# Zeros matmuls, a moved group of transposes and a swapped FFN block in the first stage of an attention and max-out FFN kernel

## The chip, the cores and the metric

The kernel runs on one core of a Trainium2 chip. The metric is device time in microseconds: the median of several executions. Besides, one execution of the kernel is recorded by the hardware profiler; the views shown here come from that execution.

## The reference

Attention with a relative-position bias, followed by a feed-forward network whose hidden layer is the largest of three products. There are 8 batches, 8 heads, 576 positions and a head width of 64; the model width is 512 and the hidden width 768.

```python
scores = scale * np.matmul(q, k.transpose(0, 1, 3, 2))
...
bias = bias_table[bucket]                      # bucket depends on |i - j| alone
scores = scores + bias.transpose(2, 0, 1)[None]
attn = np.exp(scores - max); attn = attn / (sum + 1e-09)
x = (attn @ v), as (4608 tokens, 512)
h = np.maximum(np.maximum(x @ w1, x @ w2), x @ w3)
out = h @ w_out
```

## The kernel before

Heads are taken in pairs (`hp` from 0 to 3), since two heads of width 64 fill 128 partitions. For a pair, q and k are turned (head width onto partitions) into `qT` and `kT`; `scores` (line 793) multiplies two tiles of keys with 256 queries into a PSUM tile `sc` of the pool `ps_s`, and ScalarE takes the exponential of it (`exp`, line 776) into `e4`. The bias is not added: exponentials that lie in a band around the diagonal are multiplied by the exponential of the bias (`times_band`, line 767, reading `hank`), on VectorE. The last 64 keys and queries of the 576 are handled apart (`left_keys`, `left_queries`, tile `el`). `attend` (line 876) multiplies with v, a column of ones giving the sums, and `quotients` divides. The result `x_sb` is turned into `xT`, which the FFN reads.

The pool `ps_s` has two tiles of two banks; `ps_a` and `ps_f` have two tiles of one bank each. A new tile of a pool waits until the last reader of the tile that it replaces is done.

The order of the work on TensorE is the order of the program text: the helpers `mm` and `tr` (lines 106 and 110) keep it. VectorE's copies and band products are kept in program order as well (`inorder`), and so are the transfers on the queues of SP and POOL. The exponentials on ScalarE are placed by the framework in this stage.

Batch 0 is special, because nothing is loaded yet when it begins. It is worked in two passes, both over the four pairs (from line 1048 and from line 1080). The first pass does the first 256 queries: for a pair it calls `visit` (line 811; two groups of scores, with an optional call `mid` between them), turns the q and k of the next pair (`first_transposes`, line 712: six or seven TensorE transposes into `ps_f` tiles, then two VectorE copies), casts keys from float32, runs one matmul on zeros (`keep_warm`, line 1040) and, from the second pair on, the left keys. `last_keys` (line 729) turns the tails of k for the first two pairs. Ahead of all of it stand eight matmuls on zeros (line 292) and the bias product (`spread_bias`, line 298).

The second pass does the other 320 queries, multiplies with v, and begins on the FFN of batch 0. The FFN's work is cut into portions, each a list of functions with its number of matmuls per tile; `add_ffn` (line 662) puts them into a queue, and `fill(target)` (line 677) takes portions up to the target. Where `fill` is given a hook, it runs the hook before the last function that it took. For the first 256 tokens the portions are those of line 642: `f` are the products with the first weight (`first`, line 387: eight matmuls into a `ps_f` bank, then a ScalarE copy into `hT`), `m` those with the second (`second`, line 396: eight matmuls, then a VectorE maximum), `g` those with the third. The first `fill(8)`, line 1131, takes f[0]; the one of line 1144 takes the second portion, with the turning of batch 1's first pair as its hook.

The weights, batch 1's q and k, and v go through POOL's DMA queue, in the order of the text: w1 behind batch 0's v (line 1016), then parts of batch 1, w2 (line 1027), the rest of batch 1's q and k, batch 1's v, w3 (line 1030), batch 2.

## Time and profile before

| what | value |
|---|---|
| median of 3 runs | 313.13 us (313.09, 313.13, 316.0) |
| profiled execution, its own time | 312.26 us |
| its span, first to last instruction | 310.5 us |
| busy: TensorE, VectorE, ScalarE, POOL | 96%, 67%, 65%, 36% of the span |
| mean granted TensorE clock | 0.989 |
| chain that ended last | TensorE 89%, ScalarE 5%, DMA 2% |

Times in the views are microseconds from the start of the span, so the profiled execution's own time holds 1.8 us that lie outside it. "PE" is TensorE's matmuls, "PEld" its weight loads, DVE is VectorE, ACT is ScalarE. In a timeline each row is the start, the time, the engine, the line, the operation and its tiles, and in brackets how long the engine had been idle and what ended that. Most TensorE rows carry the lines of the helpers `mm` (L107) and `tr` (L111), so they are told apart by their tiles: `warm` and `idle` are the zeros, `tp` transposes, `sc` scores, `sct` left keys, `a` the products with v, `ps` the FFN's first products.

### The profile page before, as it was taken

What the parts mean: (1) busy time and instruction counts of PE and PEld (TensorE: products, weight loads), DVE (VectorE), ACT (ScalarE), POOL (GpSimd) and SP (SyncE); (2) the same over time, 40 slices, a digit from 0 to 9 for tenths busy, and PEclk for the clock granted to TensorE, in tenths of its full rate; (3) what the DMA queues carried; (4) which work ended last, traced back from release to release, by engine and by line L of the source; (5) the groups of instructions that cost most, each with busy time, mean ns of one, the idle gap of its engine ahead of it and who ended that gap; (6) DMA issues with size and microseconds to landing.
All of it is one profiled execution on the core that took longest, in us unless ns stands there. A gap on an engine that the chain in (4) does not pass through costs nothing.

```text
span 310.5 us, 10532 instructions
## 1 busy us (share of the span) xinstructions
PE 298.9 (96%) x4542; PEld 182.5 (59%) x4542; DVE 207.7 (67%) x475; ACT 202.4 (65%) x268; POOL 110.9 (36%) x147
## 2 busy tenths in 40 slices
PE   6989999999999999999999999989999999999995
PEld 2357777775555655657665756666667654444442
DVE  7389788776777776776777667766776665553552
ACT  3899988886778777767776877675776730122211
POOL 8978752951096008900647024901500000000000
PEclk9599999999999999999999999999999999999999
DMA  9999999999999999999999999999932014202003
GB/s 167 198 187 199 182 163 136 145 166 139 141 157 191 151 187 155 133 147 198 105 101 125 165 183 111 112 146 202 131 62 106 36 33 80 101 0 103 34 0 135
DMA packets 163950, 40.48 MB, mean 130 GB/s; under 512 B 153784, under 2 KB 159424, under 8 KB 163904
## 3 DMA queue, kind: packets, MB, share of 16 engines
q0 software_dynamic: 103840, 16.66, 75.7%
q1 hardware_dynamic: 58304, 22.69, 43.6%
q8 instruction: 35, 0.57, 0.8%
q10 hardware_dynamic: 1760, 0.47, 0.7%
q14 instruction: 11, 0.09, 0.1%
HBM read 35.39 MB, written 9.45 MB: 144 GB/s over the span
## 4 chain that ended last, share of the span: by engine, by line
PE 89%; ACT 5%; DMA 2%; issue 1%; DVE 1%; ACTq 1%; DVEq 0%
PE psp L107 34%; PE ps L107 19%; PE a L107 14%; PE sc L107 9%; PE pso L107 6%; ACT e L777 4%; PE sct L107 2%; PE scq L107 2%; PE tp L111 1%; DMA xT<-in_q_dram 1%; DMA out_dram<-osb 1%; ACT el L777 1%; ACTq L213 1%; PE xp L111 0%; DVE k_sb L124 0%
## 5 line engine op out<-in xcount | busy, mean ns | idle before, releaser
L777 ACT ACTIVATE e<-sc 128x1024 bf16<-128x1024 f32 x128 | 128.4, 1023 | 30.4 <-PE sc L107 27.3
L107 PEld LDWEIGHTS <-w_bf 64*128 64x128 bf16 (+1 forms) x1088 | 73.4, 95 | 57.9 <-issue 5.0
L107 PE MATMUL psp<-xT,w_bf 64*128 64x512 bf16 x736 | 91.9, 376 | 1.9 <-issue 1.8
L771 DVE TENSOR_TENSOR e<-e,hank 128x512 bf16<-128x512 bf16 (+2 forms) x136 | 62.3, 473 | 20.3 <-ACT e L777 19.7
L107 PE MATMUL ps<-xT,w_bf 128*128 128x512 bf16 (+1 forms) x352 | 65.6, 336 | 0.0
L153 POOL DMA_DIRECT2D vx<-in_v_dram x28 | 24.7, 895 | 83.0 <-DMA kT<-k_sb 40.7
L107 PE MATMUL sc<-qT,kT 64*128 64x256 bf16 (+1 forms) x384 | 48.6, 312 | 2.0 <-DVE kT L124 0.8
L107 PEld LDWEIGHTS <-kT 64*128 64x128 bf16 (+1 forms) x736 | 31.3, 95 | 26.8 <-issue 8.4
L107 PE MATMUL a<-vx,e 64*128 64x65 bf16 (+1 forms) x1536 | 44.7, 191 | 0.0
L107 PEld LDWEIGHTS <-e 64*128 64x128 bf16 (+1 forms) x1536 | 40.7, 95 | 3.7 <-issue 0.2
L107 PEld LDWEIGHTS <-hT 64*128 64x128 bf16 (+1 forms) x444 | 26.9, 95 | 19.4 <-DVE hT L519 1.9
L107 PE MATMUL a<-vt,el 64*128 64x65 bf16 (+1 forms) x240 | 30.8, 201 | 0.4 <-DVE m L484 0.4
L107 PEld LDWEIGHTS <-el 64*128 64x128 bf16 (+1 forms) x624 | 26.2, 95 | 7.9 <-issue 4.7
L394 ACT ACTIVATE m<-ps 128x512 bf16<-128x512 f32 x14 | 8.4, 597 | 34.3 <-PE ps L107 34.3
L777 ACT ACTIVATE el<-sct 128x576 bf16<-128x576 f32 (+2 forms) x36 | 21.6, 603 | 13.5 <-PE sct L107 13.1
L107 PE MATMUL psp<-wo_bf,hT 64*128 64x256 bf16 (+1 forms) x336 | 29.7, 307 | 0.0
L181 POOL DMA_DIRECT2D q_sb<-in_q_dram x24 | 22.1, 921 | 10.7 <-issue 4.6
L181 POOL DMA_DIRECT2D k_sb<-in_k_dram x24 | 22.0, 917 | 4.0 <-DMA wo_bf<-in_moe_w_out_dram 2.1
L107 PE MATMUL pso<-wo_bf,hT 128*128 128x512 bf16 (+2 forms) x108 | 23.2, 367 | 0.0
L777 ACT ACTIVATE el<-scq 128x512 bf16<-128x512 f32 (+1 forms) x33 | 19.2, 585 | 3.3 <-PE scq L107 3.2
L403 DVE TENSOR_TENSOR m<-ps,m 128x512 bf16<-128x512 f32 x14 | 9.7, 692 | 17.0 <-PE ps L107 17.0
L519 DVE TENSOR_TENSOR hT<-psp,m 128x1024 bf16<-128x1024 f32 x12 | 14.7, 1225 | 6.9 <-PE psp L107 6.9
(82 smaller groups left out, 287.6 us busy)
## 6 DMA issues: line engine op xcount, KB each, us to landing
out_dram<-osb SPq DMA_DIRECT2D x35, 256.0 KB, 2.8
vx<-in_v_dram POOLq DMA_DIRECT2D x28, 128.0 KB, 5.0
q_sb<-in_q_dram POOLq DMA_DIRECT2D x26, 128.0 KB, 7.6
k_sb<-in_k_dram POOLq DMA_DIRECT2D x24, 128.0 KB, 7.8
w_bf<-in_moe_w_dram POOLq DMA_DIRECT2D x3, 768.0 KB, 9.3
xT<-in_k_dram SPq DMA_DIRECT2D x6, 128.0 KB, 4.2
hank<-w_dr SPq DMA_DIRECT2D x2, 384.0 KB, 5.7
wo_bf<-in_moe_w_out_dram POOLq DMA_DIRECT2D x1, 768.0 KB, 8.8
```

Of the source, the lines that this page charges most:

```text
L107: made = inorder(nc.tensor.matmul(*args, **kw))
L111: inorder(nc.tensor.transpose(*args))
L153: in_turn(b, nc.gpsimd.dma_start(out=dst[:, t, h0:h1, :], in_=x[:, t, h0:h1, :])) for t in range(t0, t1)
L181: loads.append(in_turn(b, nc.gpsimd.dma_start(out=dst[:, t], in_=main_part(src, b)[:, t])))
L213: inorder(eng.dma_start(out=dst[:, :, h, :], in_=main_part(src, 0)[:, 0:nt, h, :]))
L394: nc.scalar.activation(out=st[fb]["m0"][:], in_=ps0, func=ACTF.Copy)
L403: inorder(nc.vector.tensor_tensor(out=m[:], in0=ps1, in1=st[fb]["m0"][:], op=ALU.max))
L519: return lambda: inorder(nc.vector.tensor_tensor(out=hT[:, fb * CH : fb * CH + 2 * CH].rearrange("p (i t) -> p i t", i=2), in0=ps2(), in1= ...
L771: put(nc.vector.tensor_tensor(out=e4[:, t, :, lo:hi], in0=e4[:, t, :, lo:hi], in1=hank[:, 2 * hp : 2 * hp + 2, c0:c1][:, :, ::-1], op=ALU. ...
L777: made = nc.scalar.activation(out=out_, in_=in_, func=ACTF.Exp, scale=inv_sqrt_d)
```

## The change

The matmuls on zeros get a helper, `on_zeros(out_, n)`. At the head there are nine instead of eight; one more stands behind the first pair's transposes; `keep_warm` takes a number and runs two in the rounds of the first, second and fourth pair and one in that of the third; and the second pass begins with two, ahead of the first pair's left keys. That is seven more matmuls of 128x128 by 512.

The transposes of the third pair (`first_transposes(2)`), which stood between the second pair's two groups of scores, now follow both. Those of the fourth pair stay between the third pair's two groups, and those of the second pair stay behind the first pair's scores.

In the FFN of the first 256 tokens, f[1] goes ahead of m[0] in the second portion. The turning of batch 1's first pair stays between the two.

```diff
     warm = ps_s.tile([P, 2 * CH], F32, tag="sc", name="warm")
-    for _ in range(8):
-        mm(warm[:, 0:CH], lhsT=zeros[:, 0:P], rhs=zeros[:])
+
+    def on_zeros(out_, n=1):
+        for _ in range(n):
+            mm(out_, lhsT=zeros[:, 0:P], rhs=zeros[:])
+
+    on_zeros(warm[:, 0:CH], 9)
...
-                portions = [[f[0]], [m[0], f[1]], [m[1]], [f[2], m[2]]]
+                portions = [[f[0]], [f[1], m[0]], [m[1]], [f[2], m[2]]]
...
     first_transposes(0)
+    on_zeros(warm[:, 0:CH])
...
-    def keep_warm():
+    def keep_warm(n):
 
         idle = ps_a.tile([P, CH], F32, tag="a", name="idle")
-        mm(idle[:], lhsT=zeros[:, 0:P], rhs=zeros[:])
+        on_zeros(idle[:], n)
...
-        visit(qT, kT, e4, 0, (lambda: first_transposes(hp + 1)) if 0 < hp < HP - 1 else None)
+        visit(qT, kT, e4, 0, (lambda: first_transposes(hp + 1)) if hp == 2 else None)
         if hp == HP - 1:
             more_transposes(0)
-        if hp == 0:
-            first_transposes(1)
+        if hp < 2:
+            first_transposes(hp + 1)
...
-        keep_warm()
+        keep_warm(1 if hp == 2 else 2)
...
         if hp == 0:
+            keep_warm(2)
             keys()
```

## The prediction

> **What bounds the kernel now.** I read the page first, for the share of each engine and the granted clock. The page's second part (the span in 40 slices of 7.76 us) is cut here to the header and two rows.

> ```profile
> ## 2 busy tenths in 40 slices
> PE   6989999999999999999999999989999999999995
> ...
> PEclk9599999999999999999999999999999999999999
> ```

> TensorE is busy nearly everywhere; the one dent in its granted clock is the second slice. All that the diff touches lies before 45 us. From 68 us on the chain of waits is TensorE work end to end, so what is won before then reaches the end whole, and nothing more can be won later. The question is what sets the pace from 4 to 45 us. The windows view, cut where the clock's own records change (4.07, 7.49, 14.31 us), shows how the clock moves. Columns are length, then busy time and count of PE, PEld, DVE, ACT, POOL, then granted clock, DMA share, GB/s.

> ```profile
> 4.07:7.49 3.42, 2.28 (x20) 0.88 (x18) 2.76 (x11) 1.65 (x5) 3.42 (x6) 1.00 1.57 210
> 7.49:10.90 3.41, 2.90 (x20) 1.37 (x20) 1.48 (x6) 2.68 (x3) 3.41 (x5) 0.50 2.08 179
> 10.90:14.31 3.41, 3.41 (x23) 1.38 (x22) 1.46 (x5) 2.71 (x4) 3.41 (x6) 0.50 1.22 208
> 14.31:17.73 3.42, 2.63 (x26) 1.22 (x26) 1.79 (x7) 3.39 (x6) 2.20 (x4) 1.00 2.10 182
> ```

> So the clock is full from 4.07, half for two stretches of 3.41 us, and full again from 14.31 to the end. While it is half, ScalarE is busy 2.7 of 3.4 us; afterwards 3.39 of 3.42. The timeline of ScalarE names the gaps (start, duration, and in brackets the idle time before):

> ```profile
> 7.21 1.94 ACT L777 ACTIVATE e<-sc 128x1024 bf16<-128x1024 f32 x2 [0.61 <-PE sc L107]
> 9.68 1.02 ACT L777 ACTIVATE e<-sc 128x1024 bf16<-128x1024 f32 x1 [0.53 <-PE sc L107]
> 11.08 1.02 ACT L777 ACTIVATE e<-sc 128x1024 bf16<-128x1024 f32 x1 [0.38 <-PE sc L107]
> ...
> 14.34 1.02 ACT L777 ACTIVATE e<-sc 128x1024 bf16<-128x1024 f32 x1 [0.38 <-PE sc L107]
> 15.26 0.38 ACT L777 ACTIVATE el<-sct 128x256 bf16<-128x256 f32 x1
> 15.53 1.95 ACT L777 ACTIVATE e<-sc 128x1024 bf16<-128x1024 f32 x2
> ```

> From 15.3 to about 30 us the exponentials run back to back: ScalarE sets the pace there, and before that it waits for scores that a slow TensorE delivers late. Last I looked for the transfers that an earlier TensorE would run into, in the whole timeline of 30 to 44 us:

> ```profile
> 30.07 0.77 PEld L107 LDWEIGHTS <-w_bf 128*128 128x128 bf16 x8 [0.18 <-DMA w_bf<-in_moe_w_dram]
> ...
> 32.23 0.76 POOL L1014 DMA_DIRECT2D w_bf<-in_moe_w_dram  x1 [0.75 <-DMA xT<-in_k_dram]
> ...
> 41.83 0.88 POOL L181 DMA_DIRECT2D k_sb<-in_k_dram  x1 [1.19 <-DMA w_bf<-in_moe_w_dram]
> 41.84 0.78 PEld L107 LDWEIGHTS <-w_bf 128*128 128x128 bf16 x8
> ...
> 43.41 0.39 PE L107 MATMUL sc<-qT,kT 64*128 64x256 bf16 x4 [0.18 <-ACT el L777]
> ```

> The second weight lands just as its first product wants it (30.07). The third, issued at 32.23, lands about 9.3 us later (the tile's view gives 8.6 to 9.3 for the three weights), at 41.54, and its first product starts at 41.84: slack 0.3 us.

> **The change, part by part.** *Seven matmuls on zeros.* Starts of such matmuls are 0.43 us apart at half clock (the first eight) and a little over 0.21 at full (512 columns at twice the rate; scores of 256 columns start 0.11 apart). Where they go: one behind the eight, ending near 4.6, before the bias product that starts at 4.97; one behind the first transposes, at about 6.0, in the idle stretch up to 6.51 (TensorE waits there for kT); one each in the first and second rounds; one in the fourth, where the next scores wait for ScalarE anyway; two at the head of the second pass, where TensorE is idle from 17.7 to 18.72 behind ScalarE. At full clock all seven cost nothing, because these waits cover them. Without cover they would cost 7 x 0.21 = 1.5 us, at half clock twice that.

> Does the clock then stay full? The row first: I add up, for each stretch, issue time of the matmuls that are not transposes. 4.07 to 7.49: 0.26 (zeros) + 0.43 (bias) + 0.44 (scores) = 1.13 us, 33%, and the clock fell. 7.49 to 10.90: 0.43 + 2 x 0.43 = 1.29, 38%, and it stayed half. 10.90 to 14.31: 0.43 (zeros) + 0.43 (left keys) + 2 x 0.43 (scores) + 0.08 = 1.8, 53%, and it rose. 14.31 to 17.73: about 1.4, 41%, and it held. One line near 40% fits all four; with the transposes counted none does (72% would have stayed half and 51% held full). The change adds 2 x 0.21 to the first stretch: 1.56, 46%, above it. In the second, now at full clock, 4 zeros (0.85) and two groups of scores (0.44) make 1.29, 38%: on the line. So I expect full clock up to 10.90, and about even odds after it.

> [...] The trace shows the 3.41 us windows, but the clock fell behind a stretch with no wait over 0.7 us. [...] I follow the row.

> *What full clock and the moved transposes are worth.* I walk the first pass with the trace's own durations. The first two exponentials stay (7.21; the queue of ScalarE is issuing a store until 7.16). The second pair's k transposes start at 7.71 as before (they wait for a cast) but end at 8.10, not 8.31; copies 0.29 and 0.42 follow; scores at 8.81, ended 9.20; exponential 9.24 against 9.68. The seven transposes of the third pair no longer stand between the second pair's two groups of scores: the second group is at 9.2 (its bank is free at 9.15) instead of 10.43, and its exponential at 10.16 against 11.08, now bound by ScalarE (0.92 apart). What is late next is kT of the third pair: transposes end at 10.05, copies at 10.74, last_keys' copy at 10.97, left keys at 11.0, exponential 11.93 against 12.94, then 12.85 against 14.34. Lead of ScalarE: **about 1.4 us**. If the clock is half from 10.90, the walk gives 0.8.

> *Up to 40 us* the lead is kept. v of the first two heads lands at 13.84 and 16.84 (landing marks of its queue), and the product that reads the second one starts at 19.03, so 17.6 with the lead. The two copies that spread the next batch's q and k (DVE, 35.17) need a load that landed at 33.96: about 0.2 lost. POOL's queue does not move: it is filled eight deep and its transfers follow each other without gap from 19.5 to 41.5.

> *The swapped block.* m0 must have the second weight (30.03); with a lead of 1.4 it would wait that long. With f1 first, f1 takes the earlier slot (about 28.7), the ten transposes follow, and m0 starts at about 30.1. Both are eight matmuls of 0.11 on the same two banks; behind m0 on TensorE stand the next scores. Price 0; without the swap the lead would shrink to 0 at 30 us. f1's copy on ScalarE (0.60) may slip ahead of kT's copies (0.77): 0 to 0.6 on the path, I take 0, as tile order puts it in the wait for the transposes.

> *Where the lead goes.* The third weight still lands at 41.54, so the first product with it starts at 41.58 instead of 41.84: **0.3 us** won, over 0.9 us of lead spent waiting. Behind it on TensorE stand the next scores. In the profile before, the second group of these waits for ScalarE from 43.05 to 43.41, **0.36**. ScalarE, still ahead, has freed the bank by 41.95, so this wait vanishes. 0.3 + 0.36 = **0.66 us** stays. With a lead of 0.8 the sum is nearly the same, since 0.66 of it is all that is used.

> **The sum.** The profiled execution took 312.26 (span 310.5 and 1.8 around it); less 0.66 gives 311.6. The median shown is 313.13, 0.87 above it, so I put the forecast at **312.5**. Bounds of the unknowns: lead from -0.3 (clock half throughout) to 1.5 (all gaps of ScalarE, 0.53 + 0.38 + 0.38 and small ones); f1's copy 0 to 0.6.

> **Rivals.** (1) *The clock falls at 7.49 all the same.* Then the second round's two zeros stand in front of the left keys at 0.43 each, with only 0.16 us of cover (zeros end at 11.59, keys start at 11.75), and the moved transposes make the third kT late by 0.4, partly hidden. Exponentials of the third pair come 0.2 to 0.3 later, and ScalarE carries that on: **313.4**, slower than before. It decides if the first stretch stays under the line that I drew between 33 and 41%. For it: the line is from four stretches only. Against it: 46%.
> (2) *The third weight is no wall*, because its load is issued earlier when DVE, on which POOL waits at 17.36, is early: then the whole 1.4 stays, **311.7**. Against it: the queue has no gap to fill.
> (3) *The lead is spent before 40 us*, at the next batch's q and k (33.96) or the exchange of copies on ScalarE: **313.1**, the change does nothing that shows.

> **How the numbers follow.** Forecast 0.60, rival 1 0.20, rival 2 0.12, rival 3 0.08. The likeliest case's own range is 312.1 to 312.9. Rival 2 lies 0.8 below, and the clock's windows may lie elsewhere in other executions (one of the three runs shown is 2.9 above the others), so I go to 311.2; upward rival 1 and f1's copy (0.6) give 313.9. A measurement of this kernel tells about 1% from no change, and no case comes near 3.1 us. What I leave for either side is for windows that fall badly or well: faster 0.06, same 0.89, slower 0.05.

> **What would show it.** Right: PEclk of the second slice at 9, the exponential of 11.08 at about 10.2, idle TensorE ahead of the third weight's first product (some 1 us, released by its DMA), that product still near 41.6, and no wait for ScalarE behind it. Wrong: half clock at 8 to 10 us; first product of the third weight well before 41.5; the second weight still waited for at 30; or a wait in 45 to 68 us that was not there.

## The result, and the profile after

The changed kernel took **318.32 us** (median of six runs, 315.31 to 325.17) against 313.03 beside it on the same chip: ratio 1.0138, 95% interval 1.0094 to 1.0183. It is slower by about 1%; the forecast was 312.5 and the range ended at 313.9. Run again (the first experiment), it gave 316.59 against 314.55, ratio 1.0042 [1.0002, 1.0082]. Both intervals lie above 1, but they do not overlap: that there is a loss is clear, its size is not. The first profiled execution (325.17, span 323.4, mean granted clock 0.984) is a disturbed one, so most lines here are of a second profile of the same kernel (314.07, span 312.3, clock 0.999). That one is among its faster executions; a second profile of the kernel before (e5 below) took 314.95. So the two profiles show what moved, and not the whole price.

What the change was built around did happen. This is the windows view of the second profile, cut as before; columns are length, then busy time and count of PE, PEld, DVE, ACT, POOL, then granted clock, DMA share, GB/s:

```profile
4.07:7.49 3.42, 2.74 (x20) 0.97 (x18) 2.69 (x11) 1.66 (x5) 3.42 (x6) 1.00 1.53 217
7.49:10.90 3.41, 2.87 (x26) 1.40 (x27) 1.83 (x7) 3.11 (x4) 3.41 (x6) 1.00 2.12 175
10.90:14.31 3.41, 2.50 (x27) 1.17 (x27) 1.69 (x5) 3.15 (x7) 3.41 (x6) 1.00 1.40 170
14.31:17.73 3.42, 2.91 (x28) 1.35 (x25) 2.58 (x9) 3.42 (x6) 3.20 (x5) 1.00 1.88 216
```

The clock is full: the record's first mark is its rise at 4.57 us (the view has no value for what lies ahead of a first mark and puts 1.00). ScalarE is busy 3.11 and 3.15 us where it was busy 2.68 and 2.71. Its timeline (start, duration; in brackets the idle time before):

```profile
9.43 1.94 ACT L781 ACTIVATE e<-sc 128x1024 bf16<-128x1024 f32 x2 [0.30 <-PE sc L107]
11.62 0.66 ACT L781 ACTIVATE el<-sct 128x256 bf16<-128x256 f32 x2 [0.26 <-PE sct L107]
12.17 1.95 ACT L781 ACTIVATE e<-sc 128x1024 bf16<-128x1024 f32 x2
13.97 0.42 ACT L781 ACTIVATE el<-sct 128x256 bf16<-128x256 f32 x1
14.24 1.99 ACT L781 ACTIVATE e<-sc 128x1024 bf16<-128x1024 f32 x2
```

The exponential of 15.53 now starts at 14.24, so ScalarE leads by 1.3 us. TensorE's timeline shows where the lead ends:

```profile
41.21 1.05 PE L107 MATMUL ps<-xT,w_bf 128*128 128x256 bf16 x8 [0.61 <-DMA w_bf<-in_moe_w_dram]
42.19 0.61 PE L107 MATMUL sc<-qT,kT 64*128 64x256 bf16 x8
...
62.91 0.42 PE L107 MATMUL sct<-qT,kT 128*128 128x512 bf16 x2 [1.39 <-DMA kT<-ktail]
```

The third weight is a wall (a landing that an earlier TensorE must wait for), as forecast: TensorE waits 0.61 us there. 0.94 us of lead is left behind it. All of that goes at 62.91, where the left keys of batch 2 wait 1.39 us for the last transposed tile of its kT. It landed at 62.87; in the profile before it landed at 61.35, and the same matmuls started at 62.31 without a wait. But the kernel before has such a wait too, in its second profile, where the tile landed at 62.85. The two profiles of the kernel before, in this order:

```profile
62.31 0.41 PE L107 MATMUL sct<-qT,kT 128*128 128x512 bf16 x2
62.90 0.42 PE L107 MATMUL sct<-qT,kT 128*128 128x512 bf16 x2 [0.48 <-DMA kT<-ktail]
```

So this landing scatters by 1.5 us between executions of one kernel, and at 62.9 us the changed kernel stands level with the slower of the two.

Later there are waits that the forecast passed over. First the waits view of the kernel before (its longest line), then that of the changed kernel's second profile from 170 to 225 us, then the longest three lines of its first profile over the whole span (engine, tile, what it waited for, total us, times, longest):

```profile
PE psp L107 <- issue: 1.8, 2, 1.3
```

```profile
PE psp L107 <- issue: 2.1, 2, 1.9
PE a L107 <- DMA vt<-in_v_dram: 0.8, 2, 0.5
PE scq L107 <- issue: 0.3, 1, 0.3
```

```profile
PE a L107 <- DMA vt<-in_v_dram: 6.6, 1, 6.6
PE psp L107 <- issue: 2.8, 2, 2.4
PE scq L107 <- issue: 1.4, 1, 1.4
```

"issue" means that nothing the profile records released the instruction. These waits, which the kernel before has too, became the object of the experiments.

### The profile page after: what moved, and what is told of

Same layout as the page of the kernel before. It is cut to its first block, busy times and chain, and to the rows that moved or that the text cites. A ratio compares the mean times of both kernels' runs of the same rounds, so it can differ in the third digit from the quotient of the medians.

```text
span 323.4 us, 10533 instructions
## 1 busy us (share of the span) xinstructions
PE 301.3 (93%) x4536; PEld 183.4 (57%) x4549; DVE 207.6 (64%) x475; ACT 202.1 (63%) x268; POOL 111.0 (34%) x147
## 4 chain that ended last, share of the span: by engine, by line
PE 71%; DMA 15%; ACT 4%; DVE 3%; SPq 3%; issue 2%; POOL 1%
PE psp L107 29%; PE ps L107 15%; PE a L107 11%; PE sc L107 6%; DMA k_sb<-in_k_dram 5%; PE pso L107 4%; ACT e L781 3%; DMA vt<-in_v_dram 3%; SPq L706 3%; DMA wo_bf<-in_moe_w_out_dram 3%; PE sct L107 2%; DVE e L775 1%; DMA kT<-k_sb 1%; PE warm L107 1%; DMA qT<-qtail 1%
## 5 line engine op out<-in xcount | busy, mean ns | idle before, releaser
L107 PEld LDWEIGHTS <-w_bf 64*128 64x128 bf16 (+1 forms) x1088 | 73.7, 96 | 60.4 <-issue 7.2
L107 PE MATMUL psp<-xT,w_bf 64*128 64x512 bf16 x736 | 92.9, 381 | 2.8 <-issue 2.8
L775 DVE TENSOR_TENSOR e<-e,hank 128x512 bf16<-128x512 bf16 (+2 forms) x136 | 61.4, 466 | 21.4 <-ACT e L781 19.5
L107 PE MATMUL ps<-xT,w_bf 128*128 128x512 bf16 (+1 forms) x345 | 66.0, 337 | 1.4 <-DVE q_sb L228 0.8
L107 PE MATMUL sc<-qT,kT 64*128 64x256 bf16 (+1 forms) x384 | 47.8, 308 | 2.1 <-ACT e L781 1.1
L107 PEld LDWEIGHTS <-kT 64*128 64x128 bf16 (+1 forms) x736 | 31.2, 95 | 28.9 <-issue 10.5
L107 PE MATMUL a<-vx,e 64*128 64x65 bf16 (+1 forms) x1536 | 45.3, 191 | 0.1
L107 PEld LDWEIGHTS <-e 64*128 64x128 bf16 (+1 forms) x1536 | 41.2, 95 | 4.2 <-issue 0.3
L107 PEld LDWEIGHTS <-hT 64*128 64x128 bf16 (+1 forms) x444 | 26.9, 95 | 19.6 <-DVE hT L523 1.9
L107 PE MATMUL a<-vt,el 64*128 64x65 bf16 (+1 forms) x240 | 30.9, 202 | 7.0 <-DMA vt<-in_v_dram 6.6
L107 PEld LDWEIGHTS <-el 64*128 64x128 bf16 (+1 forms) x624 | 26.0, 95 | 14.6 <-issue 12.2
L107 PE MATMUL psp<-wo_bf,hT 64*128 64x256 bf16 (+1 forms) x336 | 29.7, 307 | 0.0
L181 POOL DMA_DIRECT2D q_sb<-in_q_dram x24 | 22.1, 920 | 9.7 <-issue 4.3
L181 POOL DMA_DIRECT2D k_sb<-in_k_dram x24 | 22.0, 917 | 8.6 <-DMA vx<-in_v_dram 4.7
L107 PE MATMUL pso<-wo_bf,hT 128*128 128x512 bf16 (+2 forms) x103 | 22.6, 367 | 0.3
L121 ACT ACTIVATE m<-psp 128x1024 bf16<-128x1024 f32 (+1 forms) x22 | 18.2, 825 | 3.5 <-PE psp L107 3.5
```

The source lines that it names most:

```text
L107: made = inorder(nc.tensor.matmul(*args, **kw))
L121: return inorder(nc.scalar.activation(out=out_, in_=in_, func=ACTF.Copy))
L181: loads.append(in_turn(b, nc.gpsimd.dma_start(out=dst[:, t], in_=main_part(src, b)[:, t])))
L775: put(nc.vector.tensor_tensor(out=e4[:, t, :, lo:hi], in0=e4[:, t, :, lo:hi], in1=hank[:, 2 * hp : 2 * hp + 2, c0:c1][:, :, ::-1], op=ALU. ...
```

## The experiments

All are timed in five rounds beside the kernel before. "Ahead" is how many TensorE instructions (weight loads and matmuls, two for each product: 4542 of each on the page before) more stand ahead of the later stages than in the kernel before. Theory I, the one that the runs bear out, says that the added instructions move all later ones against blocks of 256 of TensorE's instructions, for each of which the profile before has a packet of 16,384 bytes (35 packets, counted below).

**The parts alone.** The change itself, and three kernels with one of its parts each: the seven zeros; the moved transposes; the swap.

```
e2:  on_zeros(warm, 9) ... on_zeros(warm) ... keep_warm(1 if hp == 2 else 2) ... keep_warm(2)
e3:  visit(..., first_transposes(hp+1) if hp == 2 else None);  if hp < 2: first_transposes(hp + 1)
e4:  portions = [[f[0]], [f[1], m[0]], [m[1]], [f[2], m[2]]]
```

> The changed kernel again, to have a second execution of it in the profile. Theory A (transfers): the loads of POOL and SP are a second bound with about 2 us of slack (v of batch 3 landed at 95.9 and was wanted near 97.9 before); the change makes them later, so some 2 to 6 us are lost: 315 to 319 us, and the second profile again shows TensorE waiting for a load between 45 and 110 us. Theory B (clock): the loss is the clock's, halved behind waits: then an execution whose granted clock is above 0.995 takes 313 or less. Rival N (the executions only scatter): 313 to 314, as before.

> The seven matmuls on zeros alone, the rest as before. Theory A with the zeros as its cause (the ninth matmul at the head, at half clock, delays the bias product, so hank's transfer and what is queued behind it): 315 to 318 us, hank landing 1 us later or more. If the swapped FFN block is the cause: 312.5 to 313.5.

> The third pair's transposes behind both groups of scores, the rest as before. All theories so far: 312.8 to 313.5, as the move shifts no transfer; if it is the cause, 315 or more.

> f[1] ahead of m[0] alone, the rest as before. Theory A with the zeros as its cause: 312.8 to 313.5. Theory S (the swap is the cause: with half clock early f[1] takes the place in which the second weight has landed anyway, and copies on ScalarE and maxima on VectorE come in another order): 314.5 to 317, and the first products with the third weight start later than 41.9 although it has landed.

Measured, against 314.55: change 316.59 (ratio 1.0042 [1.0002, 1.0082]); zeros 316.27 (1.0105 [1.0045, 1.0165]); transposes 314.08 (0.9999 [0.9963, 1.0036]); swap 314.13 (0.9993 [0.9958, 1.0027]). The loss sits with the zeros; the other two parts do nothing that can be measured. Mere scatter (rival N's 313 to 314) is out. So is the clock as the whole cause (theory B): of the changed kernel's five executions with a mean granted clock above 0.995 only one took less than 313. Theory A's wait for a transfer is there (1.39 us at 62.91), but the kernel before can have it as well.

**Is it the zeros' time?** The kernel before itself, and three variants of the zeros: all seven added ones at 64 columns instead of 512; the two at the head alone; the five in the rounds and the second pass alone.

```
e6:  on_zeros(warm, 8); on_zeros(warm, 1, 64) ... on_zeros(idle, long); on_zeros(idle, n - long, 64)
e7:  on_zeros(warm, 9) ... on_zeros(warm) ... keep_warm(1)
e8:  on_zeros(warm, 8) ... keep_warm(1 if hp == 2 else 2) ... keep_warm(2)
```

> The kernel before, against itself. Every theory: a ratio of 1 within its interval, which shows how wide the scatter of this kernel is. Its profile gives the granted clock of another execution: if the clock's windows lie anyhow, it is not half from 7.5 to 14.3 us this time (most timed executions of the kernel before have a mean clock of 0.995 to 1.0), and the exponentials of the first pass come up to 1 us earlier without any change.

> The seven added matmuls on zeros at their places, but 64 columns each instead of 512: as many instructions, 0.2 us of TensorE in place of 1.5. Theory I (the added instructions shift the fetches of instructions, which take a DMA engine for 1 us, and so the loads): 316 to 317, like the full seven. Theory Z (the time of the zeros on TensorE, or what they delay, costs): 313.5 to 314.8, like before.

> Only the two added zeros matmuls ahead of the first scores. Theory H (they delay the bias product where the clock is half at the start, and with it hank's transfer): 315.5 to 317. If the rounds' five are the cause: 313.5 to 314.8.

> Only the five added zeros matmuls in the rounds and at the head of the second pass. Theory R (a TensorE held up in the rounds, or one that keeps the clock and so asks earlier for the transposed q and k of batch 2): 315.5 to 317. Theory H: 313.5 to 314.8. If the two parts share the cost, both kernels lie near 315.

Measured, against 314.11: before 313.22 (0.9978 [0.9948, 1.0008]); short zeros 317.65 (1.0098 [1.0063, 1.0133]); head 314.52 (1.0034 [1.0, 1.0068]); rounds 316.28 (1.0028 [0.999, 1.0066]). With an eighth of the columns the seven zeros cost as much as before, so it is not their time. 4 and 10 instructions ahead (head, rounds) give something between nothing and what 14 give; both intervals reach 1.

**Count or work?** Four kernels separate them: the zeros of the rounds with the head cut so that the count is that of the kernel before; seven short zeros at the head and nothing else; fourteen instructions fewer; 128 more.

```
e9:  as e2, with on_zeros(warm, 2) at the head instead of 9
e10: head: 8 long, then 7 x mm(warm[:, 0:64], lhsT=zeros[:, 0:P], rhs=zeros[:, 0:64])
e11: head: 1 long instead of 8
e12: head: 1 long and 71 short instead of 8 long
```

> The kernel before with five of the change's zeros in the rounds and the second pass and one ahead of the bias product, but with the zeros at the very head cut from eight to two, so that the program has as many TensorE instructions as before. Theory I (the 14 more TensorE instructions move all later ones against the 16 KB packets in which the instruction stream comes, and lengthen the waits that nothing releases, near 178, 192 and 208 us): from the second pass's end on the instructions stand as in the kernel before, so 313.5 to 314.5, and the gap near 208 us is 0.9 to 1.6 us. Theory R (the zeros in the rounds hold back what they stand before): 316 to 317.5 as with all seven. If the head's zeros matter for the clock, a half clock in the first 8 us and up to 1 us more than theory I has.

> The kernel before with seven more multiplications by zeros of 64 columns behind the eight at the head, none elsewhere: 14 TensorE instructions more, all before the first input is there, so they stand in nobody's way. Theory I (place in the instruction stream): 315.5 to 318, as with the change's seven zeros, with 2 us or more of waits that nothing releases near 208 us. Theory R (time or place of the zeros in the rounds): 313.5 to 314.5, no difference.

> The kernel before with one multiplication by zeros at the head instead of eight: 14 TensorE instructions fewer, the rounds untouched. Theory I: a place in the stream on the other side; the waits that nothing releases change (0.5 to 2.5 us near 208 us) and the time with them, 312 to 316. Theory R: 313.5 to 314.5, plus up to 1 us if the clock is half in the first 8 us.

> The kernel before with one long and 71 short (64 columns) multiplications by zeros at the head instead of eight long ones: 128 TensorE instructions more, half of a 16 KB packet of the stream. Theory I: every instruction of the rounds stands half a packet elsewhere, so the gap near 208 us moves by about 128 instructions' time (4 us) or goes into a place where TensorE waits anyway; time anywhere from 312 to 318. Theory R: 313.5 to 315 (1 us if the short ones end after the first input has come).

Measured, against 313.39: zeros in the rounds, same count, 313.28 (0.9991 [0.9952, 1.003]); seven short ones at the head 317.41 (1.0109 [1.0058, 1.016]); fourteen fewer 313.04 (1.0006 [0.9971, 1.0041]); 128 more 320.61 (no ratio: its six executions lie between 312.82 and 323.89; it is above theory I's 318, so that range missed). The first two decide it. Work in the rounds without a shift costs nothing that shows, and a shift without work in the rounds costs the whole 1%. (In e9 the single zeros matmul runs at 6.31 us, behind the first transposes, and not ahead of the bias product as my expectation has it.)

The traces show where the place can matter. TensorE's timelines near 208 us, for the kernel before, with the same count and with seven short zeros:

```profile
210.03 0.60 PE L107 MATMUL psp<-xT,w_bf 64*128 64x512 bf16 x3 [1.34 <-issue]
```

```profile
210.31 0.60 PE L107 MATMUL psp<-xT,w_bf 64*128 64x512 bf16 x3 [1.79 <-issue]
210.54 0.40 PE L107 MATMUL scq<-qT,kT 64*128 64x64 bf16 x5
```

```profile
208.97 0.82 PE L107 MATMUL psp<-xT,w_bf 64*128 64x512 bf16 x6
212.13 1.04 PE L107 MATMUL psp<-xT,w_bf 64*128 64x512 bf16 x8 [2.34 <-issue]
```

I counted TensorE's instructions (weight loads, matmuls and its waits for semaphores in the record) up to every wait of over 0.25 us that nothing released. In all kernels the counts are 185 to 194 modulo 256, and each such wait ends 1.2 to 2.0 us after a packet of the queue that the page before lists as

```profile
q8 instruction: 35, 0.57, 0.8%
```

has come in: 35 packets of 16,384 bytes each, one for every 256 of TensorE's instructions (the 4542 weight loads and 4542 matmuls of that page are 35.5 times 256). From these counts I take the packets for TensorE's own instructions, each packet for a block of 256, and the wait for one at the edge of a block. The edges with a wait cost 0.3 to 3.3 us each.

By this reading the length of a block is TensorE's cover for the next packet. Counted between edges and with waits taken out, it repeats to 0.01 us in the two kernels with the same shift of 14, and to 0.04 us after a shift by a whole block:

```
edge at instruction         5563  5819  6075  6331  6587  6843  7099   (us of TensorE's time before it)
same count  (e9)            6.55  5.47  4.52  7.34  7.61  5.86  4.90
14 ahead    (e10)           6.03  5.45  5.28  7.33  7.62  5.11  4.83
14 ahead    (e6)            6.03  5.46  5.28  7.33  7.62  5.11  4.82
128 ahead   (e12)           4.65  8.21  7.14  7.15  5.47  4.82  9.51
256 ahead   (e16, below)    7.61  6.59  5.46  4.52  7.34  7.61  5.86
```

At 6843 the packet starts 4.5 us after the edge before it (e9) or 4.6 (e10), takes 1.3 or 1.5, and the first instruction of the new block comes 1.9 or 1.4 later: about 7.5 us in all. The block lasts 5.86 us in one kernel and 5.11 in the other, which leaves 1.79 and 2.34. So fourteen instructions take away 0.75 us of cover there, and 0.52 at 5563. Most edges show no wait: the profile before has 35 packets and two such waits (0.46 and 1.34 us). Nor is the wait there the whole price: over the profiles the wait near 208 us is 0.9 to 1.9 us without a shift (before, e3, e4, e5, e9, e13) and 1.0 to 2.7 with 14 ahead (e1, e2, e6, e10).

**The place, or the mere number?** Four more: the whole change with the count restored; the 14 short instructions behind the late edges; shifts of 192 and 256.

```
e13: the change, with on_zeros(warm, 2) at the head instead of 9
e14: if (b, hp) == (7, 0): 7 x mm(idle[:, 0:64], lhsT=zeros[:, 0:P], rhs=zeros[:, 0:64])
e15: head: 1 long and 103 x mm(warm[0:16, 0:16], lhsT=zeros[:, 0:16], rhs=zeros[:, 0:16])
e16: head: the same with 135
```

> The whole change (five zeros in the rounds and the second pass, one ahead of the bias product, the transposes moved, the swap), but with two zeros at the head instead of nine, so that TensorE has as many instructions as in the kernel before. Theory I (the place of the later instructions against the 256-instruction packets makes the time): 312.5 to 313.8, no difference from before. Rival W (the whole change costs something beside its 14 instructions): 315 to 317.5, as the change itself.

> The kernel before with seven short multiplications by zeros at the start of the last batch's first pair (TensorE instructions 7177 to 7190, behind the packet edges near 178, 208 and 216 us): 14 more instructions in all, as in the run with seven short ones at the head, but none of them ahead of the late packets. Theory I (place): 313.3 to 314.2 (0.2 us of work and up to 0.7 us for the bank they write), gap near 208 us 1.3 to 1.9 us as before. Rival N (the mere number or size of the program): 316 to 318.

> The kernel before with one long and 103 very short (16 x 16) multiplications by zeros at the head instead of eight long ones: 192 TensorE instructions more, so every later instruction stands 192 further along, which against packets of 256 is the same as 64 back. Theory I with a period of 256: no less late packets, other places: 311 to 318, and the gap that is now near 208 us stands 64 instructions later in the program than in the kernel before. Rival M (the more instructions ahead, the longer the waits): above 320. Up to 1.5 us more than either if the short ones end after the first input is there.

> As the run with 192 more, but with 135 very short ones: 256 TensorE instructions more, one whole packet. Theory I with a period of 256: every later instruction stands where it stood in its packet, so the waits that nothing releases come at the same instructions as before (0.9 to 1.9 us near 208 us) and the time is that of the kernel before plus what the longer head costs, 313 to 315. Rival M (the more instructions ahead, the longer the waits): above 320.

Measured, against 313.81: whole change with the count restored 314.88 (1.0024 [0.9982, 1.0066]); late 314.12 (1.0044 [1.0014, 1.0075]); 192 ahead 314.46 (1.0036 [1.0002, 1.007]); 256 ahead 314.3 (1.0015 [0.9981, 1.0049]). Rival M (more is worse) and rival N (the number) asked for 316 or above and fall. The late ones still cost 0.4%, clear of no change; 0.2 to 0.9 us had been allowed for their own work and bank. The restored change is not so clear: 314.88 misses theory I's 312.5 to 313.8 as well as rival W's 315 to 317.5, and its interval holds the 1.0042 that the change itself gave in e1. In the executions with a mean granted clock of 0.999 or more it takes 313.6 us (5 of them) against 315.4 for the change in e1 (5), which speaks for theory I. The longer head is no rival: with 256 ahead the bias product starts at 5.19 us, later than with seven short zeros (5.09; 4.97 and 4.81 in the kernel before), and costs nothing that shows. The shift by 256 repeats the kernel before, one block later. In the table its times are those of the same count one edge on; TensorE's timeline has the same products behind its wait, at the edge 7099:

```profile
213.27 0.60 PE L107 MATMUL psp<-xT,w_bf 64*128 64x512 bf16 x3 [1.28 <-issue]
213.50 0.40 PE L107 MATMUL scq<-qT,kT 64*128 64x64 bf16 x5
```

At 192 the waits are elsewhere: 1.52 us at 4027, 0.75 at 4283, 2.12 at 5563 (178 us), and none near 208 us. My expectation for that run named the old gap, 64 instructions later in the program; that was wrong, since another block stands there, with another length.

**Why is the packet late?** The last two kernels leave out q's and k's loads for the last two batches, whose scores are made of tiles of earlier batches; TensorE's work stays as it is (4542 weight loads with and without the loads). One has the seven short zeros ahead, one has not.

```
e17, e18:  if hp == 2 and 4 <= b < B - 2: batch[b + 2] = batch[b]     # no load_tiles, no load_qk
```

> The kernel before with seven more short multiplications by zeros at the head, and without the loads of q and k of the last two batches (22 of GpSimd's transfers are left out; the last two batches' scores are made of the fifth and sixth batches' tiles, with as much work on every engine). Theory T (the instruction packets come late because the loads' small packets keep the DMA engines full at 160 to 178 and at 194 to 211 us): the packets ahead of 179 and 209 us start earlier, the gaps there fall from 0.9 and 2.3 us to under 0.4 us, and the time falls by 2 to 3.5 us from that of the same kernel with its loads, to 313.5 to 315.5; within 0.4% of the run without the short ones. Rival Q (the packets are asked for late whatever the traffic): the gaps stay, 316 to 318.

> The kernel before without the loads of q and k of the last two batches (left out as in the run with the short ones). Theory T: the gaps of 1.0 and 1.6 us near 179 and 208 us fall to under 0.4 us each, 311 to 312.5. Rival Q: they stay, 313 to 314.

Measured, against 312.75: with the short zeros 311.6 (0.996 [0.9922, 0.9998]), without 309.48 (0.9906 [0.9874, 0.9938]). Both are below what was expected (313.5 to 315.5 and 311 to 312.5). Waits view of the run without the short zeros, 20 to 300 us, all that is above 0.15 us:

```profile
PE scq L107 <- ACT e L777: 0.7, 3, 0.3
PE a L107 <- DVE m L484: 0.4, 1, 0.4
PE sc L107 <- ACT el L777: 0.2, 1, 0.2
```

No "issue" is among them. The packets for the edges 5563 and 6843 now start 0.6 and 1.0 us after the edge before (with loads, in e9, 4.0 and 4.5), that is, soon after TensorE enters the block whose successor they bring. The windows of the kernel before (its second profile, e5) and of this one (columns as above) show the transfers beside them:

```profile
200.00:209.00 9.00, 9.00 (x196) 6.18 (x193) 6.51 (x12) 6.41 (x9) 4.04 (x6) 1.00 2.67 149
209.00:212.00 3.00, 1.86 (x17) 0.72 (x13) 1.16 (x4) 1.95 (x3) 0.00 (x0) 1.00 1.49 102
```

```profile
200.00:209.00 9.00, 9.00 (x188) 6.21 (x186) 5.40 (x12) 6.61 (x9) 0.00 (x0) 1.00 0.85 161
209.00:212.00 3.00, 3.00 (x110) 2.39 (x107) 2.71 (x5) 1.89 (x2) 0.43 (x1) 1.00 0.38 57
```

A DMA share of 2.67 (more than all the engines' time, by the sum of what packets took) falls to 0.85, and TensorE is busy 3.00 of 3.00 us where it was busy 1.86. Theory T's loads are thereby shown to be what makes the packets late, rival Q's fixed request excluded. (With the loads GpSimd's issuing of them is gone too; the two were not taken apart.) Another number missed: the two runs were to be within 0.4% and are 2.1 us (0.7%) apart, where with loads the short ones cost 4.0 us (317.41 against 313.39). By these medians about half of the shift's price is not in the stretches that the two kernels relieve. In the few executions with a mean granted clock of 0.999 or more they take 310.7 and 310.2 us.

**What stays open.** I added up TensorE's waits above 0.03 us from 20 us on. Six profiles with no shift there (before, e3, e4, e5, e9, e13) have 3.4 to 6.4 us, mean 5.4; four with 14 ahead (e1, e2, e6, e10) have 7.1 to 8.8, mean 7.6. Of these 2.3 us more, 0.3 is "issue" and 1.7 is waits for transfers (kT of batch 2, v, the weights), both with much scatter between executions. A second part is the clock: half stretches of 3.4 to 6.8 us follow some of the long waits (below). The timed executions say how much: with a mean granted clock of 0.999 or more, those without a shift (the kernel before and the five runs named) take 313.5 us on average (95 of them), those with 14 ahead (the change, e1, e2, e6, e10) 315.7 (15); below that clock the averages are 314.8 (104) and 318.8 (27). So about 2.2 us of the loss are there at full clock, and the rest comes with a lower one. That the place in the stream costs the time is shown, and that late packets cost time at the edges. How the shift comes to make the waits for data transfers longer was not tried and stays open.

## Why the prediction was wrong

- **Clock full, lead of 1.4 us by 16 us:** came true (1.3, and 1.43 at 31.65). In all four profiles with both head zeros at full length (two of the change, e2, e7) the clock, once up, stays full to 20 us; in five of seven with eight zeros at the head (before, e4, e5, e8, e18, but not e3 and e14) it is half for a stretch before 15 us. But it buys nothing at the end: e9, with two zeros at the head, issues scores at half rate (0.18 to 0.21 us apart, against 0.11 at full clock in the profile before) until its clock rises at 11.04, and takes 313.28. The rise itself varies between the profiles: with eight zeros it is at 4.07 to 5.05 or at 13.5 to 13.8 us. My line near 40%, drawn through four stretches of one execution, was not needed and is not shown.
- **Swap at price 0:** e4 0.9993. Right.
- **POOL's queue does not move:** not contradicted. The second weight landed at 29.20 instead of 30.03, the third at 41.17 instead of 41.54, which is rival 2's direction without its size; but in the profiles without a shift these landings lie anywhere from 29.25 to 30.31 and from 41.13 to 41.85.
- **The third weight a wall, 0.66 us kept:** right in kind; 0.94 was kept to 60 us (exponential 59.82 for 60.76), of which 0.37 is the weight's earlier landing.
- **"From 68 us on the chain of waits is TensorE work end to end", nothing more won or lost:** the step that failed. There were two mistakes in it. Batch 2's kT is a second wall before 68 us, with 0.96 us of slack in the one profile that I had (landed 61.35, wanted 62.31) and none in the next (62.85). And after it TensorE's chain holds the edges of its own instruction blocks, which added instructions move: 1.8 us of "issue" in the profile before, 1.9 to 4.6 in the ten profiles compared above.
- **Seven zeros "cost nothing, because these waits cover them":** the term that was mis-sized. Their time does cost nothing (e9 0.9991). Their 14 places in the stream cost 4.0 us in e10 (317.41 against 313.39), more than the 1.5 us that I gave them without any cover; of these 4.0 us the edges explain a part, and the rest stays open.
- **Rivals:** the slow one (clock falls anyway, 313.4) had the right side for a wrong reason; none of the four cases had a place after 45 us.

The hint was in view: the profile before has 1.8 us of "issue" ahead of the `psp` products, all of it in two waits, and a queue named instruction. The prediction shows neither.

## What to carry to other kernels

In this long unrolled program, with a DMA share of 2.67 between 200 and 209 us (e5), 14 more TensorE instructions cost 4.0 us by themselves (e10, 317.41 against 313.39). In a program like it, try a change in their count as a change of its own, with as many instructions taken out elsewhere (here, at the head), before the edit itself is judged. It is worth counting the instructions up to a wait with no releaser on a busy engine, modulo the block that the packets suggest (here 256), and laying the wait beside the instruction queue's packets. Padding is no cure: none of the shifts tried beat the kernel before. Less load traffic in stretches where TensorE's instructions are dense is worth trying: leaving out 22 loads was worth 3.3 us. Larger load packets, or the same loads at another time, were not tried.

## What the runs showed of the hardware

```profile
210.52:213.01 2.49, 0.00 (x0) 0.00 (x0) 0.00 (x0) 0.61 (x1) 0.00 (x0) 1.00 1.81 95
213.01:216.43 3.42, 2.63 (x31) 2.01 (x32) 1.51 (x3) 0.34 (x1) 0.00 (x0) 0.50 1.07 282
216.43:219.84 3.41, 3.41 (x26) 2.00 (x22) 1.32 (x3) 1.22 (x2) 0.00 (x0) 0.50 0.78 145
```

The two half stretches begin 2.49 us into the wait. Of their 6.8 us TensorE is busy 6.04 at half its rate, which is some 3.0 us of its time (an estimate from these rows): about as much again as the wait. In this execution, then, the half clock that came with the wait cost about what the wait did.
